# More loads ahead, twelve transfers on another queue, and one multiplication earlier: a recurrent-attention and two-layer kernel on one core

## The chip, the core and the metric

The kernel runs on one core of a Trainium2 chip. The metric is device time in microseconds (us), less is better. A core has five engines that matter here: TensorE (PE) multiplies matrices; VectorE (DVE), ScalarE (ACT) and GpSimd (POOL) do elementwise work; SyncE (SP) does nothing here but issue transfers. Each engine takes its instructions strictly in the order in which the program gives them to it, and waits at semaphores for the others.

## The reference, cut to what matters

Four sequences of 768 steps with 8 heads of width 48 go through a linear attention with a decaying state, and its output (3072 tokens of 384 features) through two feed-forward layers:

```python
for t in range(S):                                   # S = 768
    cur = einsum('bhd,bhe->bhde', u * k[t], v[t])
    y[t] = einsum('bhd,bhde->bhe', r[t], state + cur)
    state = w * state + einsum('bhd,bhe->bhde', k[t], v[t])
x = y as (3072, 384)
x = (sigmoid(x @ w_gate) * (x @ w_val)) @ w_out      # 384 -> 1536 -> 384
x = relu(x @ w_in) ** 2 @ w2_out                     # 384 -> 2048 -> 384
```

The layers' weights are float64. The kernel turns each of them into float32 parts on the chip.

## The kernel before, in words

**Steps and units.** The 768 positions are cut into six steps of 128, and step c of sequence b is a unit, n = 4c + b. There are 24. One unit's attention is a set of small matmuls with work around it: `attn_pre` (r times k times u, two POOL instructions, lines 232 and 233), `attn_prep` (k and r times powers of w, two DVE instructions, line 241), `attn_sum` (DVE), `attn_diag` (eight small ACT instructions, line 257), `attn_kh` (k times a table, one POOL instruction, line 264; from step 3 on DVE does it), `attn_mask` (DVE, line 328), `attn_mid` and `attn_state` (DVE, lines 403 to 414), and `attn_out`. `attn_out(n)` has the output matmuls of unit n, then the scores and the sums (k as `attn_kh` left it, times v) of unit n + 1, then two ACT copies of those sums (`us`, line 336) and two of the output (`ys`, line 384), and transfers of `ys` into `xr`, the layer's input (lines 386 to 392): two a unit, and four more at the last unit of a step, twelve a step. SP issues them.

**Phases.** Step 0's attention runs first, by itself. Then the first layer runs over step 0 for its first seven column blocks (phase 0), over steps 1 to 5 for all twelve, and over step 0 for the other five; then the second layer over all steps. While phase i runs, the attention of step i + 1 is woven in: `unit_ops` lays the operations of its four units into numbered slots, three to a column block, and `fill` runs the operations of one slot. A column block f is a gate product (`pg`), a value product (`pv`), line 445, and, one block later, an output product (line 464). Each phase starts with three ACT casts of `xr` (`xh`, line 432) and three DVE subtractions (`xl`, line 428).

**Weights.** 68 weight tiles of 384 KB are turned into float32 parts by `convert`. Call n does: an ACT cast and a POOL subtraction for tile n - 2 (lines 135 and 136), a DVE combination for tile n - 1 (line 148), an ACT and a DVE instruction on tile n (lines 156 and 158), and then asks SP for a tile that goes into the buffer which line 148 has just read. With `NRB` buffers that is tile n + NRB - 1. Four calls stand before phase 0, and in phases 0 and 1 nearly every slot ends with one.

**Order of loads.** SP's queue carries the loads too. A unit has four pieces, 1 MB together. At the start SP is given the units 0 to 4 and the weight tiles 0 to 3. Unit 5 (`B + 1`) comes after step 0's attention, and so behind step 0's twelve `xr` transfers on SP's queue. The units 6, 7 and 8 are asked for in `attn_out(4)`, behind the weight tiles that the calls of `convert` before it asked for.

Of the kernel before, what the change touches and what calls it, by code (L numbers as in the profile page):

```python
# [19 lines left out]
B, H, S, D = 4, 8, 768, 48  # L20
# [6 lines left out]
KT = DM // P  # L27
# [15 lines left out]
def tile_kernel(  # L43
# [18 lines left out]
    dp = ctx.enter_context(tc.tile_pool(name="dp", bufs=1, space=bass.MemoryType.DRAM))  # L62
    pp = ctx.enter_context(tc.tile_pool(name="pp", bufs=1, space=PSUM))

    NRB = 4
    NW = 36
    IN_W = 8
    CUT = 7
# [159 lines left out]
    def attn_pre(n):  # L228
        if n >= NU:
            return  # L230
        rn = rn_t[n]
        side(n).tensor_tensor(out=rn, in0=rn, in1=kv_t[n][:, HD:], op=ALU.mult)
        side(n).tensor_tensor(out=rn, in0=rn, in1=u_bc, op=ALU.mult)

    def attn_prep(n):
        if n >= NU:
            return
        two = trk.unsqueeze(2).to_broadcast([DP, HP, 2, L])
        for t in (k_t[n], r_t[n]):
            t = t.rearrange("p j (a t) -> p j a t", a=2)  # L240
            nc.vector.tensor_mul(t, t, two)
# [17 lines left out]
    def attn_kh(n):  # L259

        if n >= NU:
            return
        k = kv_t[n][:, HD:]
        side(n).tensor_tensor(out=k, in0=k, in1=th, op=ALU.mult)  # L264
# [75 lines left out]
    def attn_out(n):  # L340
        c, b = units[n]
        kv, am = kv_t[n], am_t.pop(n)
        opened.clear()

        def mm(a, q, j, m, lhsT, rhs):
            mm64(2 * a, q, (y1, y2)[a][64 * q : 64 * q + m, j * L : (j + 1) * L], lhsT, rhs)

        def reads(second):

            for j in range(HP):  # L350
                for q in range(2):
                    h = head(q, j)
                    a = h % 2 ^ second
                    o = slice(64 * (h % 2), 64 * (h % 2) + D)
                    if a or c:
                        st = mid_t[n][o, j] if a else state[o, b, j]
                        mm(a, q, j, D, st, r_t[n][o, j, a * L : (a + 1) * L])

        if n + 1 < B:
            attn_scores(n + 1)  # L360
        for j in range(HP):
            for q in range(2):
                h = head(q, j)
                for a in range(2):
                    x = slice(a * L, (a + 1) * L)
                    mm(a, q, j, width[q], kv[x, h * D :][:, : width[q]], am[x, h])
        reads(0)
        settle(kv)
        if n >= B:
            attn_scores(n + 1)  # L370
        if n != B - 1:
            attn_sums(n + 1)
        settle(kv)
        reads(1)
        while n >= B and len(kv_t) <= n + (4 if len(kv_t) < IN_W + 2 else 3) and len(kv_t) < NU:
            load_unit(len(kv_t))
        if n != B - 1:
            attn_us(n + 1)
        if b == 0:
            bank["y"] = sp.tile([P, B, HP, C], F32, tag="ys", name="ys", bufs=1)  # L380
            xraw[c] = sp.tile([P, KT, B, C], F32, tag="xraw", name="xr", bufs=1)
        ys = bank["y"]
        for a, y in enumerate((y1, y2)):
            nc.scalar.copy(ys[0:DP, b, :, a * L : (a + 1) * L], y[0:DP].rearrange("p (j t) -> p j t", j=HP))
        x = xraw[c]
        nc.sync.dma_start(out=x[0:48, :, b], in_=ys[0:48, b, 0:KT])
        nc.sync.dma_start(out=x[48:96, :, b], in_=ys[64:112, b, 0:KT])
        if b == B - 1:
            nc.sync.dma_start(out=x[96:128, 0], in_=ys[0:32, :, KT])
            nc.sync.dma_start(out=x[96:112, 1], in_=ys[32:48, :, KT])  # L390
            nc.sync.dma_start(out=x[112:128, 1], in_=ys[64:80, :, KT])
            nc.sync.dma_start(out=x[96:128, 2], in_=ys[80:112, :, KT])

    decay = wdec.unsqueeze(2).to_broadcast([DP, HP, D])

# [78 lines left out]
    def unit_ops(c, tiles):  # L474


        starts = (0, 9, 18, 27, 36) if tiles == F1 else (3, 8, 12, 17, 21)
        slots = [[] for _ in range(3 * tiles)]
        if c == 1:
            slots[0].append(lambda: (attn_pre(B + 1), attn_prep(B + 1)))  # L480
            slots[1].append(lambda: (attn_kh(B + 1), attn_sum(B + 1)))
            slots[2].append(lambda: (attn_diag(B + 1, 0), attn_diag(B + 1, 1)))
        for b in range(B):
            n = c * B + b
            ops = [
                lambda n=n: attn_out(n),
                lambda n=n: (attn_mask(n + 1), attn_mid(n + 1)),
                lambda n=n: (attn_state(n), attn_pre(n + 2)),
                lambda n=n: attn_prep(n + 2),
                lambda n=n: attn_sum(n + 2),  # L490
                lambda n=n: attn_diag(n + 2, 0),
                lambda n=n: attn_diag(n + 2, 1),
                lambda n=n: attn_kh(n + 2),
            ]
            s0, room = starts[b], starts[b + 1] - starts[b]
            for i, op in enumerate(ops):
                slots[s0 + i * room // len(ops)].append(op)
        return slots
# [114 lines left out]
    with tc.manual_schedule():  # L613
        nc.vector.memset(idle, 0.0)
        warm(WARM0)
        nc.vector.memset(seven, 0.0)
        nc.scalar.activation(seven, seven, AF.Sigmoid)
        nc.sync.dma_start(out=w_sb, in_=wt)
        id_sb = sp.tile([DP, D], F32, tag="ev", name="id_sb", bufs=2)
        maskf = sp.tile([C, L], F32, tag="ev", name="maskf", bufs=2)  # L620
        nc.sync.dma_start(out=id_sb, in_=ident)
        load_unit(0)
        nc.sync.dma_start(out=anti, in_=antid)
        nc.sync.dma_start(out=maskf, in_=mask)
        load_unit(1)
        load_unit(2)
        load_raw(0)
        load_unit(3)
        load_raw(1)
        load_raw(2)  # L630
        load_unit(4)
        load_raw(3)
        powers = tables()
        attn_pre(0)
        nc.gpsimd.tensor_copy(mask8, maskf)
        attn_pre(1)
        attn_prep(0)
        state_tables(*powers)
        attn_scores(0)
        attn_sum(0)  # L640
        attn_diag(0, 0)
        attn_diag(0, 1)
        attn_kh(0)
        attn_kh(1)
        attn_prep(1)
        attn_mask(0)
        attn_sum(1)
        attn_diag(1, 0)
        attn_sums(0)
        attn_us(0)  # L650
        attn_diag(1, 1)
        for n in range(B):
            m = n + 2
            if m < B:
                attn_pre(m)
                attn_kh(m)
                attn_prep(m)
            warm(WARM_OUT[n])
            attn_out(n)
            if m <= B:  # L660
                attn_mask(n + 1)
            if m < B:
                attn_sum(m)
                attn_diag(m, 0)
                attn_diag(m, 1)
            if n in (1, 2):
                convert()

        load_unit(B + 1)
        attn_pre(B)  # L670
        attn_kh(B)
        attn_prep(B)
        attn_sum(B)
        attn_diag(B, 0)
        attn_diag(B, 1)
        warm(WARM_X[0])
        attn_scores(B)
        attn_sums(B)
        attn_us(B)
        convert()  # L680
        convert()
        warm(WARM_X[1])
        for k in range(KT):
            x_from(0, k)
        attn_mask(B)
        attn_mid(B)
        for i, (layer, c, f0, f1) in enumerate(phases):
            ops = unit_ops(i + 1, f1 - f0) if i + 1 < NCH else []
            slot = 0

            def fill(f, j):

                nonlocal slot
                for op in ops[slot] if ops else []:
                    op()
                slot += 1
                lim = 0
                if i == 0:
                    lim = 3 * CUT + 2
                elif i == 1:  # L700
                    base = 3 * CUT + 2
                    lim = min(base + slot * (3 * F1 + 2 - base) // 27, 3 * F1 + 2)
                elif i == NCH - 1 and j < 2:
                    lim = min(3 * F1 + 3 * f - 2, 3 * F1 + 3 * CUT + 1)
                elif i == REDO and j < 2:
                    lim = 3 * F1 + 3 * f - 2
                elif i == REDO + 1 and j == 2:
                    lim = NWQ + 2
                for _ in range(2 if i == 0 and slot == 1 else 1):
                    if wn[0] < lim:  # L710
                        convert()

            for f in range(f0, f1):
                while (layer, f, 1) not in wunit:
                    convert()
                inner(i, f, fill)
        finish()
# [68 lines left out]
```

## Time and profile before

| | us |
|---|---|
| median of 3 runs | 977.85 (976.94 to 978.19) |
| the profiled execution | 979.93 |
| its span in the trace | 978.1 |
| PE busy in the span | 947.2 (97%) |
| DVE, ACT, POOL busy | 450.8, 402.9, 132.4 |
| transfers | 76.86 MB, mean 79 GB/s |

PE is busy for 97% of the span, but not evenly: its tenths in the first five of forty slices are 7, 7, 8, 8, 8, and DVE's 5, 6, 7, 7, 7 where the later slices have 3 or 4. [...] A row of the timeline gives the start, the duration, the engine, the line and the operation, and in brackets the time for which the engine stood idle before it and what released it.

### The profile page before, as it was taken

The numbers are of one execution on the slowest core, as the hardware profiler recorded it, in microseconds if no ns is written. First come the engines' busy times: TensorE is split into PE (matmuls) and PEld (weight loads), VectorE is DVE, ScalarE is ACT, GpSimd is POOL, SyncE is SP. The second block draws the span as 40 slices with busy tenths as digits, with TensorE's granted clock in tenths as the row PEclk, the third lists the DMA queues.
The fourth block names the chain that finished last, engine by engine and source line by source line (L and its number), as shares of the span: only waits on it lengthen the run. The fifth ranks groups of instructions, "written<-read, shape, count | busy, mean of one in ns | idle before, by whom it ended". The sixth has DMA issues, their size and how long they took to land.

```text
span 978.1 us, 16626 instructions
## 1 busy us (share of the span) xinstructions
PE 947.2 (97%) x6898; PEld 757.1 (77%) x6898; DVE 450.8 (46%) x742; ACT 402.9 (41%) x826; POOL 132.4 (14%) x121
## 2 busy tenths in 40 slices
PE   7788899999999999999999999999999999999997
PEld 4466678888888888887888888888888888888886
DVE  5677756754344345423344364433433433434332
ACT  3765565533333323322466463332422322323322
POOL 7455544200000000000133121000000000000000
PEclk7987999999999999999999999999999999999999
DMA  8674545532122222001244540010100100100000
GB/s 305 179 254 140 157 151 153 172 92 64 53 61 85 66 87 88 18 8 44 90 125 127 162 130 1 1 64 1 38 28 1 65 0 1 65 1 1 32 1 33
DMA packets 42235, 76.86 MB, mean 79 GB/s; under 512 B 5168, under 2 KB 17584, under 8 KB 42160
## 3 DMA queue, kind: packets, MB, share of 16 engines
q1 hardware_dynamic: 42160, 75.80, 24.5%
q8 instruction: 54, 0.88, 0.4%
q14 instruction: 21, 0.17, 0.1%
HBM read 60.05 MB, written 11.01 MB: 73 GB/s over the span
## 4 chain that ended last, share of the span: by engine, by line
PE 89%; DVE 2%; DMA 2%; POOL 2%; ACT 1%; SPq 1%; issue 1%; DVEq 0%; POOLq 0%; ACTq 0%
PE pg L445 35%; PE two L464 16%; PE pv L445 15%; PE po L464 12%; PE att L464 7%; PE att L272 4%; DMA first<-in_rkv 2%; SPq L104 1%; DMA xr<-ys 0%; POOL wu L136 0%; POOL gl L428 0%; ACT am L257 0%; ACT raw L156 0%; PE pw L611 0%; POOL first L264 0%
## 5 line engine op out<-in xcount | busy, mean ns | idle before, releaser
L445 PE MATMUL pg<-xh,wu 128*128 128x512 f32 x1008 | 318.3, 400 | 6.5 <-ACT wu L135 3.1
L445 PEld LDWEIGHTS pg<-xh,wu 128*128 128x128 f32 x1008 | 191.0, 190 | 55.6 <-ACT wu L135 3.6
L445 PE MATMUL pg<-xl,wu 128*128 128x512 f32 x504 | 196.7, 398 | 0.3 <-DVE xl L428 0.2
L597 ACT CAST gh<-s 128x512 fp32r<-128x512 f32 (+1 forms) x169 | 104.7, 620 | 192.5 <-DVE s L593 119.0
L596 DVE TENSOR_TENSOR s<-s 128x512 f32<-128x512 f32 (+1 forms) x97 | 66.6, 687 | 181.5 <-ACT s L595 181.5
L428 DVE TENSOR_TENSOR gl<-s,gh 128x512 fp32r<-128x512 f32 x162 | 111.5, 688 | 78.1 <-PE po L464 57.7
L464 PE MATMUL two<-gh,wu 128*128 128x512 f32 x472 | 147.3, 393 | 0.0
L445 PE MATMUL pv<-xh,wu 128*128 128x512 f32 x432 | 141.2, 408 | 1.5 <-POOL wu L136 1.4
L593 DVE TENSOR_TENSOR s<-pv,s 128x512 f32<-128x512 f32 x72 | 49.6, 689 | 197.4 <-PE pv L445 193.8
L595 ACT ACTIVATE s<-pg 128x512 f32<-128x512 f32 (+1 forms) x97 | 57.6, 594 | 190.4 <-PE pg L445 190.4
L445 PEld LDWEIGHTS pg<-xl,wu 128*128 128x128 f32 x504 | 95.9, 190 | 23.7 <-DVE xl L428 1.1
L464 PE MATMUL po<-gh,wu 128*128 128x512 f32 (+1 forms) x338 | 105.4, 392 | 0.0
L464 PEld LDWEIGHTS two<-gh,wu 128*128 128x128 f32 x472 | 88.8, 189 | 21.4
L445 PEld LDWEIGHTS pv<-xh,wu 128*128 128x128 f32 x432 | 81.4, 192 | 22.8 <-POOL wu L136 2.1
L464 PE MATMUL two<-gl,wu 128*128 128x512 f32 x236 | 92.5, 392 | 0.0
L579 ACT ACTIVATE s<-pg 128x512 f32<-128x512 f32 x72 | 43.8, 608 | 112.6 <-PE pg L445 112.5
L445 PE MATMUL pv<-xl,wu 128*128 128x512 f32 x216 | 86.1, 399 | 0.0
L464 PEld LDWEIGHTS po<-gh,wu 128*128 128x128 f32 x338 | 63.4, 188 | 14.8
L156 ACT ACTIVATE raw<-raw 128x384 bf16<-128x384 bf16 x68 | 73.6, 1082 | 0.0
L464 PE MATMUL po<-gl,wu 128*128 128x512 f32 (+1 forms) x169 | 66.2, 392 | 0.0
L464 PE MATMUL att<-gh,wu 128*128 128x512 f32 (+1 forms) x204 | 63.4, 392 | 0.0
L464 PEld LDWEIGHTS two<-gl,wu 128*128 128x128 f32 x236 | 44.2, 187 | 10.0 <-POOL gl L428 0.3
(298 smaller groups left out, 922.5 us busy)
## 6 DMA issues: line engine op xcount, KB each, us to landing
raw<-in_w SPq DMA_DIRECT2D x68, 384.0 KB, 3.1
kv<-in_rkv SPq DMA_DIRECT2D x16, 384.0 KB, 3.6
xin<-x2d SPq DMA_DIRECT2D x6, 768.0 KB, 4.2
out<-x2s SPq DMA_DIRECT2D x18, 256.0 KB, 2.1
first<-in_rkv SPq DMA_DIRECT2D x16, 256.0 KB, 5.5
kT<-in_rkv SPq DMA_DIRECT2D x16, 256.0 KB, 4.6
rT<-in_rkv SPq DMA_DIRECT2D x16, 256.0 KB, 5.0
x2d<-x2s SPq DMA_DIRECT2D x15, 256.0 KB, 2.0
```

Of the source, the lines that this page charges most:

```text
L104: nc.sync.dma_start(out=got[i][0], in_=got[i][1])
L156: nc.scalar.activation(top, top, AF.Prelu, scale=2.0**-112, alpha=2.0**32)
L272: nc.tensor.matmul(out, lhsT=lhsT, rhs=rhs, start=(bank, q) not in opened, stop=True, skip_group_check=True)
L428: (eng or nc.vector).tensor_tensor(out=dst, in0=src, in1=high.bitcast(F32), op=ALU.subtract)
L445: nc.tensor.matmul(ps, lhsT=a, rhs=b_, start=(i == 0), stop=(i == len(pairs) - 1))
L464: nc.tensor.matmul(po[k][:, ts], lhsT=a, rhs=b_[:, ts], start=(first and m == 0), stop=(last and m == 2 and ts is cuts[-1]),)
L579: nc.scalar.activation(s, pg, AF.Sigmoid)
L593: nc.vector.tensor_tensor(out=s[:, ts], in0=pv[:, ts], in1=s[:, ts], op=ALU.mult)
L595: nc.scalar.activation(s[:, ts], pg[:, ts], AF.Relu)
L596: nc.vector.tensor_mul(s[:, ts], s[:, ts], s[:, ts])
L597: nc.scalar.copy(gh[:, ts], s[:, ts])
```

## The change

The diff has four parts. Weight tiles get seven buffers in place of four, so `convert` asks for tile n + 6 in place of n + 3. The loads at the start take in unit 5 and the weight tiles 4, 5 and 6. Step 0's twelve `xr` transfers are issued from ScalarE's queue, in program order right behind the `ys` copies that they read; the other steps' stay with SP. And `attn_kh` of a unit moves ahead of its `attn_prep`: from the last of the unit's eight places in the slots to the fourth, one place behind `attn_pre`, and for unit 5 from slot 1 to slot 0.

```diff
-    NRB = 4
+    NRB = 7
...
         x = xraw[c]
-        nc.sync.dma_start(out=x[0:48, :, b], in_=ys[0:48, b, 0:KT])
-        nc.sync.dma_start(out=x[48:96, :, b], in_=ys[64:112, b, 0:KT])
+
+        eng = nc.sync if c else nc.scalar
+        eng.dma_start(out=x[0:48, :, b], in_=ys[0:48, b, 0:KT])
+        eng.dma_start(out=x[48:96, :, b], in_=ys[64:112, b, 0:KT])
         if b == B - 1:
-            nc.sync.dma_start(out=x[96:128, 0], in_=ys[0:32, :, KT])
...
+            eng.dma_start(out=x[96:128, 0], in_=ys[0:32, :, KT])
...
         if c == 1:
-            slots[0].append(lambda: (attn_pre(B + 1), attn_prep(B + 1)))
-            slots[1].append(lambda: (attn_kh(B + 1), attn_sum(B + 1)))
+            slots[0].append(lambda: (attn_pre(B + 1), attn_kh(B + 1), attn_prep(B + 1)))
+            slots[1].append(lambda: attn_sum(B + 1))
...
                 lambda n=n: (attn_state(n), attn_pre(n + 2)),
-                lambda n=n: attn_prep(n + 2),
+                lambda n=n: (attn_kh(n + 2), attn_prep(n + 2)),
                 lambda n=n: attn_sum(n + 2),
                 lambda n=n: attn_diag(n + 2, 0),
                 lambda n=n: attn_diag(n + 2, 1),
-                lambda n=n: attn_kh(n + 2),
+                lambda: None,
...
         load_raw(3)
+        load_unit(B + 1)
+        for n in range(4, NRB):
+            load_raw(n)
         powers = tables()
...
-        load_unit(B + 1)
         attn_pre(B)
```

## Rows read from the trace of the kernel before

**Rows 1.** Windows: stretch, length, busy us of PE to POOL, clock, DMA, GB/s.
```profile
22.17:37.31 15.14, 14.08 (x382) 8.83 (x380) 7.57 (x15) 14.21 (x46) 5.04 (x6) 1.00 0.39 104
37.31:117.81 80.50, 64.33 (x717) 49.56 (x717) 61.12 (x90) 47.43 (x105) 48.09 (x40) 0.85 0.67 208
117.81:130.00 12.19, 10.24 (x155) 7.37 (x156) 4.70 (x10) 5.08 (x16) 2.22 (x2) 0.86 0.28 91
130.00:450.00 320.00, 319.90 (x3166) 259.75 (x3165) 157.21 (x282) 125.65 (x304) 27.00 (x21) 1.00 0.27 81
```

**Rows 2.** Timeline of PE, rows ahead of which it stood idle.
```profile
46.23 0.50 PE L445 MATMUL pg<-xh,wu 128*128 128x512 f32 x1 [3.13 <-ACT wu L135]
48.09 0.79 PE L445 MATMUL pg<-xh,wu 128*128 128x512 f32 x1 [1.36 <-POOL wu L136]
...
72.21 1.09 PE L272 MATMUL att<-first 64*64 64x48 f32 x32 [1.88 <-POOL first L264]
...
89.75 1.09 PE L272 MATMUL att<-first 64*64 64x48 f32 x32 [3.88 <-POOL first L264]
...
124.66 0.67 PE L272 MATMUL att<-kv 64*64 64x48 f32 x32 [1.60 <-POOL kv L264]
```

**Rows 3.** Chain of waits that ended last: start, us, what.
```profile
37.86 4.85 DMA first<-in_rkv
...
53.53 6.11 DMA first<-in_rkv
...
111.78 4.79 DMA xr<-ys
...
125.63 3.82 PE pv L445 x9
...
139.94 2.10 PE pv L445 x9
```

**Rows 4.** Timeline of ACT: the first cast, and the `us` copies in phase 0.
```profile
37.31 1.73 ACT L432 CAST xh<-xr 128x512 fp32r<-128x512 f32 x3
...
55.35 0.54 ACT L336 COPY us<-att 112x192 f32<-112x192 f32 x2 [0.95 <-PE att L272]
...
73.97 0.54 ACT L336 COPY us<-att 112x192 f32<-112x192 f32 x2 [1.08 <-PE att L272]
...
91.51 0.54 ACT L336 COPY us<-att 112x192 f32<-112x192 f32 x2 [1.88 <-PE att L272]
...
108.84 0.54 ACT L336 COPY us<-att 112x192 f32<-112x192 f32 x2 [0.38 <-PE att L272]
```

**Rows 5.** Instructions on the tile `xr`: count, ns min/median/max, first and last start.
```profile
L387 SPq DMA_DIRECT2D xr<-ys x24: 594/599/1153, 24.1 to 447.3; - x24
```

**Rows 6.** Instructions on the tile `raw`, same columns.
```profile
L122 SPq DMA_DIRECT2D raw<-in_w x68: 327/328/1659, 10.1 to 576.8; - x68
```

**Rows 7.** Instructions of line 136, same columns: POOL's sequencer.
```profile
L136 POOLq EVENT_SEMAPHORE  x50: 17/17/330, 30.0 to 592.5; - x50
```

**Rows 8.** Timeline of DVE in phase 0.
```profile
42.73 2.43 DVE L241 TENSOR_TENSOR first<-first,trk 112x512 f32<-112x512 f32 x2 [0.73 <-DMA first<-in_rkv]
...
62.19 3.18 DVE L241 TENSOR_TENSOR first<-first,trk 112x512 f32<-112x512 f32 x2
...
98.79 0.68 DVE L241 TENSOR_TENSOR kT<-kT,trk 112x512 f32<-112x512 f32 x1
...
106.73 1.41 DVE L148 SCALAR_TENSOR_TENSOR wt__1405<-raw 128x384 int32<-128x384 int32 x1 [0.84 <-ACT raw L156]
```

**Rows 9.** Timeline of POOL: `attn_pre` of units 5 and 6.
```profile
42.19 1.03 POOL L232 TENSOR_TENSOR first<-first 128x384 f32<-128x384 f32 x1 [4.41 <-DMA first<-in_rkv]
...
59.70 1.26 POOL L232 TENSOR_TENSOR first<-first 128x384 f32<-128x384 f32 x1 [1.75 <-DMA first<-in_rkv]
```

**Rows 10.** Instructions of line 264 (`attn_kh`), columns as in rows 5.
```profile
L264 POOL TENSOR_TENSOR first<-first,th x8: 993/1008/1441, 13.5 to 88.4; 128x384 f32<-128x384 f32 x8
```

More of the change, by code (lines that the diff above doesn't have):

```diff
@@ L385, in attn_out @@
         x = xraw[c]
-        nc.sync.dma_start(out=x[0:48, :, b], in_=ys[0:48, b, 0:KT])
-        nc.sync.dma_start(out=x[48:96, :, b], in_=ys[64:112, b, 0:KT])
+        eng = nc.sync if c else nc.scalar
+        eng.dma_start(out=x[0:48, :, b], in_=ys[0:48, b, 0:KT])
+        eng.dma_start(out=x[48:96, :, b], in_=ys[64:112, b, 0:KT])
         if b == B - 1:
-            nc.sync.dma_start(out=x[96:128, 0], in_=ys[0:32, :, KT])
-            nc.sync.dma_start(out=x[96:112, 1], in_=ys[32:48, :, KT])
-            nc.sync.dma_start(out=x[112:128, 1], in_=ys[64:80, :, KT])
-            nc.sync.dma_start(out=x[96:128, 2], in_=ys[80:112, :, KT])
+            eng.dma_start(out=x[96:128, 0], in_=ys[0:32, :, KT])
+            eng.dma_start(out=x[96:112, 1], in_=ys[32:48, :, KT])
+            eng.dma_start(out=x[112:128, 1], in_=ys[64:80, :, KT])
+            eng.dma_start(out=x[96:128, 2], in_=ys[80:112, :, KT])
     decay = wdec.unsqueeze(2).to_broadcast([DP, HP, D])
```

## The prediction, made blind

> **What bounds the kernel now.** I read the windows first, then the rows ahead of which PE stood idle, the chain of waits, and last the timelines of ACT, DVE and POOL. From 130 to 450 us PE is busy for 319.9 of 320.0 us at the full clock [rows 1]; it runs matmuls that the change does not touch, and so do the windows behind. There nothing on another engine, no load and no place of `attn_kh` can move the end. What the change can win or lose lies ahead of 130 us. There PE is not the bound: phase 0, from the first cast `xh` at 37.31 [rows 4] to phase 1's first product at 117.81, takes 80.5 us, of which PE is busy 64.3, and at a mean clock of 0.85, with DVE busy 61.1 and POOL 48.1 [rows 1]. PE's gaps have names: block 1 waits for its weights, 3.13 and 1.36 us; the sums of units 6, 7 and 9 wait for `attn_kh`, 1.88, 3.88 and 1.60 us [rows 2]. But a gap of PE is worth only what the engine that feeds it next gives back, so the sum goes by the chain through DVE, ACT and POOL, not by adding PE's gaps.
>
> Step 0's attention has a bound of its own: between 22.17 and 37.31 ACT is busy 14.21 of 15.14 us [rows 1], and the first cast starts the moment ACT is through, without a wait [rows 4].
>
> **Step 0's transfers on ACT's queue.** Twelve issues leave SP and enter ACT, each right behind the `ys` copy whose result it sends. A transfer of this shape holds SP for 0.60 us (median of 24, shortest 0.594) wherever it stands [rows 5]. No row shows ACT issuing one. Bounds: at the least what a sequencer's own instruction takes, 0.017 us [rows 7], or 0.2 in all; at the most the longest such issue, 1.153 [rows 5], or 13.8. Between them lies a plain weight load's 0.327 [rows 6], or 3.9. I take 0.60, the same instruction on another sequencer: 7.2 us. ACT has 0.93 us of idle in the stretch (15.14 less 14.21) that can take some: +6.3 us on the first cast, which goes from 37.3 to about 43.6. What is queued behind the issues on ACT: the diagonals of units 2, 3 and 4, the `us` copies, the casts of the first weight tiles, and the three `xh`; `attn_mask` on DVE waits for the diagonals, PE for the masks. SP loses as much, but SP has nothing left there that is due.
>
> [...]
>
> [...]
>
> **Unit 5 and three weight tiles at the start.** Seven more transfers, 2.2 MB, go behind the others on SP's queue, so they delay none of the earlier ones. In the stretch behind, the DMA engines are used 39% at 104 GB/s [rows 1], so they land long before they are read. What goes is unit 5's load on the chain, 4.85 us [rows 3], for which POOL stood idle 4.41 us [rows 9] and DVE 0.73 [rows 8]. DVE then did two instructions in 2.43 us that take 0.68 each when undisturbed [rows 8]: 0.73 + 2.43 - 1.36 = 1.8 us earlier for the DVE work behind. POOL's share, `attn_pre(5)` and now `attn_kh(5)`, is done before phase 0 starts. Bounds: 0 (DVE is held up by another wait) to 4.5 (both PE gaps of block 1). I take 1.8, since DVE's order runs on. Late next: unit 6's load, which goes out behind weight tiles and takes 6.11 us [rows 3]; POOL waits 1.75 for it [rows 9].
>
> **Seven buffers** I cost at nothing: a load still waits for the same line 148, only three tiles further ahead. No wait for a weight tile stands in the rows; without that cover it is one issue, 0.33 us [rows 6], and a transfer.
>
> **`attn_kh` earlier.** The sums no longer wait for it, so `us` comes earlier. ACT was idle for PE ahead of `us` 0.95, 1.08, 1.88 and 0.38 us [rows 4], 4.3 in all; more than that PE's earlier finish cannot give ACT. Bounds: 0 to 4.3. I take all, since `attn_kh` or unit 5 stood behind each of them. Against it: each `attn_kh`, 1.0 us [rows 10], is now on POOL ahead of the weight subtraction and beside `attn_prep` on DVE. Such neighbours show a price: two of line 241 took 3.18 us, where alone one takes 0.68 [rows 8]. [...] Three units at 1.0 would be 3.0, nothing if the old price comes back whole; I take 2.0. In phase 0 then 1.8 + 4.3 - 2.0 = 4.1 us won, and phase 1's casts, which wait for SP's transfers of step 1 (4.79 us, [rows 3]), move with it, as those transfers follow the same chain.
>
> In phase 1 unit 9's `attn_kh` runs on an idle POOL. The gap of 1.60 [rows 2] goes, and with it, I think, the low clock behind: 3.82 less 2.10 for the nine products there [rows 3], 1.7. Together 3.3; bounds 1.6 and 3.3. From then on PE is the bound, so this counts in full. From phase 2 on, the move lies under full PE [rows 1]: nothing.
>
> **Sum.** +6.3 - 4.1 - 3.3 = -1.1 us: span 978.1 to 977.0. The profiled execution, 979.93, has 1.8 us around its span; the median of the runs, 977.85, lies 2.1 under it. I apply the difference to the median: 976.8.
>
> **Rivals.**
> 1. ACT's issues are cheap. For: a sequencer's own instruction takes 0.017 us [rows 7]. Against: SP's 0.60. At 0.017 the +6.3 vanishes: -7.4, 970.4. At 0.327: 3.9 - 0.9 = +3.0, so -4.4, 973.4. [...]
> 2. Slower: unit 6's load takes the place of unit 5's. Place: `attn_pre(6)` on POOL, 1.75 us idle already [rows 9]. If the chain gets there 1.8 + 0.95 = 2.75 us sooner but the load lands no sooner after the first cast than now (53.53 + 6.11 = 59.64 [rows 3] against 37.31, 22.3 us), POOL waits 4.5, the 2.75 are lost, and `attn_kh(6)` puts 1.0 more ahead of the weight subtraction that PE's next product needs. Phase 0 then gives 0.35 and the sum is +6.3 - 0.35 - 3.3 = +2.65: 980.5. If the low clock in phase 1 also stays, 982.2. It decides once phase 0 gives back less than 1 us. For: the load is asked for behind the same line 148 as before. Against: that instruction moves up too, and unit 5's megabyte no longer shares the engines with it.
> 3. ACT's issues are dearer than SP's: at 1.153 us the sum is +12.9 - 7.4 = +5.5, 983.3. Against: only one issue of that length.
>
> **How the numbers follow.** Chances: my forecast 0.47, by itself 974 to 979.5; rival 1 0.25; rivals 2 and 3 together 0.28. About 0.2% (2 us) is what a measurement of this kernel can tell from no change. Faster by more: rival 1 and 0.19 of the forecast's 0.47, 0.44. Within: 0.2 of the forecast and 0.05 of rival 2, 0.25. Slower: the rest, 0.31. The range takes in rival 1 at its cheapest and rival 2, and reaches towards rival 3: 970 to 983.
>
> **What would show it.** On ACT's queue, twelve transfers of `xr` at about 0.6 us each, the first `xh` at 43 to 45 us. Line 241 for unit 5 without a wait, two in about 1.4 us. No PE gap released by line 264 behind 40 us. POOL's wait ahead of `attn_pre(6)` no longer than 2 us (rival 2: over 4). From first `xh` to PE's start in phase 1 about 76 us in place of 80.5, and a clock above 0.86 in the twelve microseconds behind that. Wrong: `xh` before 40 us (rival 1) or after 47 (rival 3), or phase 0 that takes 80 us again.

## The result: 6.7 us slower, where 1 us faster was forecast

| | us |
|---|---|
| median before, 4 runs | 978.02 (976.94 to 980.15) |
| median after, 4 runs | 984.85 (983.1 to 986.72) |
| ratio | 1.0068 (95% interval 1.0047 to 1.0089) |
| profiled execution of after, its span | 984.52, 982.7 |

The time lies outside the range of the prediction, above it. The windows of after, cut at the places that answer to those of [rows 1] (first `us` copy, first cast `xh`, phase 1's first product, the 12.19 us behind it, the steady part); the clock column is the clock granted to PE, as a share of the full one:

```profile
23.03:47.29 24.26, 16.31 (x377) 10.33 (x380) 8.34 (x15) 14.27 (x46) 5.23 (x5) 0.86 0.59 180
47.29:124.87 77.58, 61.58 (x716) 45.59 (x716) 61.47 (x90) 46.84 (x105) 48.38 (x41) 0.91 0.62 194
124.87:137.06 12.19, 12.14 (x166) 8.90 (x166) 6.99 (x16) 7.11 (x20) 2.19 (x2) 0.86 0.35 111
137.06:457.06 320.00, 319.90 (x3165) 259.58 (x3164) 155.95 (x276) 123.19 (x301) 27.79 (x21) 1.00 0.27 81
```

Step 0's attention, from the first `us` copy to the first `xh`, takes 24.26 us in place of 15.14, at the same ACT busy time (14.27 against 14.21, [rows 1]): the twelve issues are not counted as busy time, but ACT computes nothing while it issues them. Phase 0 takes 77.58 in place of 80.50, and PE has hardly a gap in the 12.19 us behind it (12.14 busy, 10.24 before). The steady part has not moved.

ACT's timeline of after, from unit 2's second transfer to the first cast (`ACTq` is ACT issuing):

```profile
34.38 1.22 ACTq L389 DMA_DIRECT2D xr<-ys  x1
35.65 1.06 ACT L156 ACTIVATE raw<-raw 128x384 bf16<-128x384 bf16 x1 [1.96 <-issue]
36.45 0.72 ACT L384 COPY ys<-att 112x256 f32<-112x256 f32 x2
37.21 0.59 ACTq L388 DMA_DIRECT2D xr<-ys  x1
37.84 0.61 ACTq L389 DMA_DIRECT2D xr<-ys  x1
38.76 0.61 ACTq L391 DMA_DIRECT2D xr<-ys  x1
39.42 0.67 ACTq L392 DMA_DIRECT2D xr<-ys  x1
40.13 1.63 ACTq L393 DMA_DIRECT2D xr<-ys  x1
41.80 0.61 ACTq L394 DMA_DIRECT2D xr<-ys  x1
42.46 2.02 ACT L257 ACTIVATE am<-anti,dv 128x64 f32<-128x64 f32 x8 [5.28 <-DMA xr<-ys]
...
47.29 1.71 ACT L434 CAST xh<-xr 128x512 fp32r<-128x512 f32 x3
```

Eight of the twelve issues take 0.59 to 0.63 us, SP's price in [rows 5]; the others take 0.67, 0.69, 1.22 and 1.63, 9.1 in all. Between unit 3's second issue (done at 38.45) and the third ACT waits 0.31 us. The chain of waits says for what:

```profile
33.71 5.03 DMA xr<-ys
```

The issue at 38.76 was released by the landing of a transfer that ACT had itself asked for at 33.71. SP's waits between 10 and 60 us show that SP waits for ACT's transfers too (columns: who waited for whom, us in total, times, longest):

```profile
SPq L122 <- DMA xr<-ys: 14.7, 5, 6.2
```

The weight loads on SP now wait for ACT's transfers; the longest of these waits, 6.2 us, ends with tile 3's load. SP's timeline shows what that does to the early loads, first before, then after (weight tile 3, and in after unit 5 behind it):

```profile
17.79 0.33 SPq L122 DMA_DIRECT2D raw<-in_w  x1
```

```profile
26.49 0.33 SPq L122 DMA_DIRECT2D raw<-in_w  x1
27.12 2.83 SPq L104 DMA_DIRECT2D first<-in_rkv  x4
```

With the transfers left on SP the same two stand at 18.24 and 18.91. So in the changed kernel the loads added at the start are not early: they go out from 27.12 us on, and from 24 to 26 us the share of the DMA engines is 0.15, where it is 1.06 with the transfers left on SP.

In the compiled program 244 of the changed kernel's 293 transfers wait, besides for their data, for the completion of an earlier transfer, on one of eight completion semaphores; ACT's twelve use seven of the eight that SP's 281 use. With the transfers alone moved it is 228 of 293, all twelve of ACT's among them (four of its issues):

```
L387 DMA xr<-ys 48x3x128 [waits DMAHW6_49,Activation_49]
L388 DMA xr<-ys 48x3x128 [waits DMAHW0_49]
L390 DMA xr<-ys 32x4x128 [waits DMAHW2_49]
L391 DMA xr<-ys 16x4x128 [waits DMAHW4_49]
```

PE's rows that answer to [rows 2]:

```profile
48.02 3.11 PE L447 MATMUL pg<-xh,wu 128*128 128x512 f32 x6 [4.37 <-ACT xh L434]
57.33 0.50 PE L447 MATMUL pg<-xh,wu 128*128 128x512 f32 x1 [2.50 <-ACT wu L135]
74.02 0.50 PE L447 MATMUL pv<-xh,wu 128*128 128x512 f32 x1 [2.28 <-POOL wu L136]
106.61 0.79 PE L447 MATMUL pv<-xh,wu 128*128 128x512 f32 x1 [3.74 <-ACT wu L135]
```

No gap is released by line 264 (`attn_kh`) any more. But other gaps are there, released by the weights' cast and subtraction, with 3.74 us as the longest, where 3.88 by line 264 was the longest in [rows 2].

DVE and POOL at the start of phase 0, against [rows 8] and [rows 9], POOL's rows first:

```profile
47.68 1.11 POOL L232 TENSOR_TENSOR first<-first 128x384 f32<-128x384 f32 x1
48.87 1.34 POOL L233 TENSOR_TENSOR first<-first,u_bc 128x384 f32<-128x384 f32 x1
50.17 1.45 POOL L264 TENSOR_TENSOR first<-first,th 128x384 f32<-128x384 f32 x1
```

```profile
48.00 4.17 DVE L430 TENSOR_TENSOR xl<-xr,xh 128x512 fp32r<-128x512 f32 x3
...
54.99 1.28 DVE L241 TENSOR_TENSOR first<-first,trk 112x512 f32<-112x512 f32 x2
56.19 0.54 DVE L148 SCALAR_TENSOR_TENSOR wt__731<-raw 128x384 int32<-128x384 int32 x1
```

Line 241 for unit 5 runs without a wait, two in 1.28 us, as forecast. POOL's three instructions for unit 5 were not done early, though: they stand in its order behind the two weight subtractions of the prologue, and now run beside the three `xl` subtractions of DVE, which take 4.17 us, where before they took 1.90.

### The profile page after: what moved, and what is told of

Its sections match the earlier page's. It is cut to its first block, busy times and chain, and to the rows that moved or that the text cites. A ratio compares the mean times of both kernels' runs of the same rounds, so it can differ in the third digit from the quotient of the medians.

```text
span 982.7 us, 16600 instructions
## 1 busy us (share of the span) xinstructions
PE 944.7 (96%) x6892; PEld 753.8 (77%) x6898; DVE 452.5 (46%) x742; ACT 401.9 (41%) x826; POOL 133.6 (14%) x121
## 4 chain that ended last, share of the span: by engine, by line
PE 88%; ACT 4%; DVE 3%; DMA 1%; issue 1%; SPq 1%; ACTq 1%; POOL 0%; DVEq 0%; POOLq 0%
PE pg L447 35%; PE two L466 16%; PE pv L447 15%; PE po L466 12%; PE att L466 7%; PE att L272 4%; ACT am L257 1%; ACT raw L156 1%; DMA xr<-ys 1%; DVE first L241 1%; DMA first<-in_rkv 1%; DVE state L415 0%; ACT ys L384 0%; DVE mid L406 0%; ACT wu L135 0%
## 5 line engine op out<-in xcount | busy, mean ns | idle before, releaser
L257 ACT ACTIVATE am<-anti,dv 128x64 f32<-128x64 f32 x192 | 49.8, 335 | 13.8 <-DVE dv L247 5.8
```

What stands on the lines that cost most here:

```text
L257: nc.scalar.mul(am_t[n][:, h], anti, dv_t[n][:, h : h + 1])
```

## The experiments

All are compared with runs of the kernel before on the same chip. Differences in us are the ratio less one, times the median before (977.8 to 978.3).

**The transfers alone on ACT's queue.**

```diff
+        eng = nc.sync if c else nc.scalar
-        nc.sync.dma_start(out=x[0:48, :, b], ...)
+        eng.dma_start(out=x[0:48, :, b], ...)        # and the other five lines
```

> The kernel before with step 0's twelve transfers on ACT's queue and nothing else. Theory 1 (each issue holds ACT about 0.75 us, and ACT bounds step 0's attention): first xh 8 to 10 us later than in the kernel before, on ACT's queue 12 issues with a sum near 9 us; the whole slower by 6 to 9 us, less than the cast's delay because unit 5's load no longer stands behind these transfers on SP. Rival (the loads added at the start collide with ACT's transfers, the issues alone are cheap): first xh at most 4 us later, the whole within 3 us of the kernel before.

Measured: 986.57, ratio 1.0086 (1.0069 to 1.0103), +8.4 us. This is inside theory 1's range. The twelve issues take 7.8 us together; the first `xh` comes at 46.73, and ACT does no work for 5.39 us ahead of the diagonals behind the last six. There ACT also waits ahead of two of the last six issues, 0.99 us before 38.78 and 0.55 before 41.25:

```profile
38.78 0.61 ACTq L390 DMA_DIRECT2D xr<-ys  x1
...
41.25 0.59 ACTq L393 DMA_DIRECT2D xr<-ys  x1
```

This part alone accounts for the whole loss (6.7, and the intervals overlap).

**Only the first six of them.**

```diff
+        eng = nc.scalar if c == 0 and b < B - 1 else nc.sync
```

> The kernel before with only the six transfers of units 0 to 2 of step 0 on ScalarE's queue, the six of unit 3 on SyncE's as before. All twelve cost 8.4 us by themselves. Theory 1 (each issue holds ScalarE for its 0.59 to 0.70 us in a stretch where ScalarE has less than a microsecond to spare, so the cost goes with their number): six issues of about 0.63 us are 3.8 us, less 0.9 of idle time at most: 2.9 to 3.8 us slower than before, first cast xh 3 to 4 us later. Rival (only the six that stand directly ahead of the casts count, with the wait that they put ahead of the cast; the early ones are hidden, since ScalarE waits for TensorE there anyway): 0 to 1.5 us slower.

Measured: 983.42, ratio 1.0049 (1.0034 to 1.0064), +4.8 us. The cost goes with the number of issues, 0.7 to 0.8 us for each; the early ones are not hidden, so the rival is refuted. It is above the upper end of theory 1's range, which held issue time alone.

**ACT held for the same time, without transfers.**

```diff
+        for _ in range((6 if b == B - 1 else 2) if c == 0 else 0):
+            nc.scalar.copy(spare, spare)
```

> The kernel before, all transfers on SyncE's queue, with twelve extra copies of a spare tile of 128x512 on ScalarE (0.57 us each, by the casts xh of that shape) where the twelve issues stood: two behind each of units 0 to 2, six behind unit 3. They compute nothing that is used. Theory 1 (ScalarE's own time is the whole cost: 12 x 0.57 = 6.9 us less 0 to 0.9 of idle time): 6 to 7.5 us slower than before, about 0.9 of the 8.4 that the issues cost. Rival (a third or more of the cost is the second queue: waits for completion lanes and transfers that land later): 4 to 5.5 us slower.

Measured: 983.37, ratio 1.0055 (1.0041 to 1.0069), +5.4 us; the first `xh` at 42.92. The copies took 7.7 us in all, the issues 7.8. ACT's rows, six copies where the last six issues stood:

```profile
34.32 3.87 ACT L387 COPY spare<-spare 128x512 f32<-128x512 f32 x6
38.09 2.01 ACT L257 ACTIVATE am<-anti,dv 128x64 f32<-128x64 f32 x8
```

ACT goes from the copies to the diagonals in 3.87 us here, without a gap; with six issues in their place that was 5.39 us (transfers alone) and 5.28 (after). So about 5.4 of the 8.4 us is what holding ACT costs, and 3 us, by the difference, come with real issues; the two intervals touch, so the split is rough. The rival had the better size, but not all of the 3 us is waiting for the second queue. In the two traces 1.5 us of it are the two waits ahead of an issue, and 0.4 is one issue of 1.03 us; the rest is that an issue starts when the `ys` copy ahead of it has ended (unit 0's at 23.66 us, the copy's end at 23.62), where the spare copy starts a little before that (22.71 against 22.84).

**The change with the transfers left on SP.** It is the changed kernel with one line set back:

```diff
-        eng = nc.sync if c else nc.scalar
+        eng = nc.sync
```

> The changed kernel with step 0's transfers back on SP; loads and attn_kh as changed. Theory 1: first xh within 1 us of the kernel before (37.3), phase 0 shorter by 3 to 4 us, 2 us won in phase 1: 971 to 974 us, so 11 to 13 us less than the changed kernel. Rival (the slowness comes from the loads or from attn_kh's place): still above 978.

Measured: 977.81, ratio 1.0003 (0.9991 to 1.0016). The expectation was missed: the rest of the change isn't worth 4 to 7 us but nothing, and the first `xh` comes at 40.28, not within 1 us of 37.3. Some part of it costs.

**`attn_kh` earlier, alone.**

```diff
-                lambda n=n: attn_prep(n + 2),
+                lambda n=n: (attn_kh(n + 2), attn_prep(n + 2)),
...
-                lambda n=n: attn_kh(n + 2),
+                lambda: None,
```

(and unit 5's from slot 1 to slot 0, as in the change.)

> The kernel before with attn_kh moved alone. My prediction's terms: 4.3 less 2.0 in phase 0 and 3.3 in phase 1, 5.6 us in all; by what the changed kernel's trace shows rather 3 to 4: 973 to 975. [...]

Measured: 974.73, ratio 0.997 (0.9958 to 0.9982), -2.9 us (1.8 to 4.1 faster): the smaller size that was expected, and about half of the 5.6 of the prediction's terms.

**`attn_kh` earlier for unit 9 alone.**

```diff
+                lambda n=n: (n + 2 == 9 and attn_kh(9), attn_prep(n + 2)),
...
+                lambda n=n: n + 2 != 9 and attn_kh(n + 2),
```

> The kernel before with the multiplication of k for unit 9 alone two slots earlier, units 5 to 8 where they were. All five units together won 2.9 us. By the prediction's terms unit 9 wins the gap of 1.6 us and 1.7 us of low clock in phase 1, 3.3 us, and the others 2.3: then this kernel is 3 us faster than before and the others brought nothing. Rival (TensorE's order around the gap gives back part: only the gap itself goes, and units 5 to 8 won the rest): 1 to 1.6 us faster than before.

Measured: 975.86, ratio 0.9976 (0.9966 to 0.9985), -2.3 us (1.5 to 3.3 faster): between the two expectations, and by the medians' ratios most of the 2.9. The intervals overlap widely, so what units 5 to 8 bring can't be told from nothing by the times. PE's timelines show why it is so little. First the kernel with unit 9 alone moved, then the one with all five:

```profile
88.66 1.09 PE L272 MATMUL att<-first 64*64 64x48 f32 x32 [3.71 <-POOL first L264]
...
99.33 0.50 PE L445 MATMUL pv<-xh,wu 128*128 128x512 f32 x1 [0.38 <-POOL wu L136]
```

```profile
37.40 2.23 PE L445 MATMUL pg<-xh,wu 128*128 128x512 f32 x6 [0.92 <-ACT xh L432]
...
91.00 0.49 PE L445 MATMUL pg<-xh,wu 128*128 128x512 f32 x1 [0.46 <-POOL wu L136]
96.87 0.80 PE L445 MATMUL pv<-xh,wu 128*128 128x512 f32 x1 [3.74 <-ACT wu L135]
```

The gap of 3.71 us by `attn_kh` goes, and eight microseconds later stands a gap of 3.74 by the weights, where there was one of 0.38 (one product later). PE now does the work behind the old gap earlier, and waits for weights that come hardly earlier: ACT's cast of this tile starts 59.66 us behind the first `xh`, against 60.01.

**Buffers and early loads, alone.**

```diff
-    NRB = 4
+    NRB = 7
...
         load_raw(3)
+        load_unit(B + 1)
+        for n in range(4, NRB):
+            load_raw(n)
```

> The kernel before with seven buffers and the early loads alone. My prediction's term: 1.8 us. 975 to 977. Rival (unit 6's load takes the place of unit 5's, so nothing is won): 977.5 to 978.5. First xh unchanged by both.

Measured: 980.34, ratio 1.0024 (1.001 to 1.0038), +2.4 us: slower, against both theories. PE's timeline shows two gaps that before does not have, each in the middle of a group of like matmuls, with no releaser ("issue": it waited for nothing that the profile shows), and the window between them the count of what PE did (matmuls, weight loads):

```profile
26.99 0.63 PE L272 MATMUL pa<-first 48*64 48x64 f32 x28 [0.88 <-issue]
...
32.41 0.57 PE L272 MATMUL att<-am,first 64*48 64x64 f32 x25 [1.35 <-issue]
```

```profile
26.98:32.40 5.42, 3.75 (x127) 2.65 (x127) 3.96 (x8) 3.98 (x11) 0.00 (x0) 1.00 0.81 252
```

DMA in two-microsecond windows, first of this kernel, then of the one with `attn_kh` alone (the last two columns: share of the DMA engines, GB/s):

```profile
24.00:26.00 2.00, 2.00 (x50) 1.23 (x45) 1.31 (x3) 1.72 (x8) 1.92 (x3) 1.00 1.04 387
26.00:28.00 2.00, 1.12 (x67) 1.01 (x66) 0.90 (x2) 2.00 (x10) 0.67 (x1) 1.00 1.04 397
28.00:30.00 2.00, 1.90 (x66) 1.43 (x59) 1.78 (x4) 1.32 (x3) 0.00 (x0) 1.00 1.09 335
```

```profile
24.00:26.00 2.00, 2.00 (x64) 1.26 (x59) 1.44 (x3) 1.71 (x8) 1.92 (x3) 1.00 0.36 89
```

With the early loads the DMA engines are full to about 30 us (a share of 1.04 to 1.09 up to there, 0.45 behind), without them to about 23 (1.04 from 20 to 22 us, 0.80 from 22 to 24). The profiled executions are single ones, and their whole times don't follow the medians (978.04 here, 979.93 before): the stretches in which PE is granted half of the full clock fall differently in each (from 37.31 to 117.81 us the mean is 0.91 here, 0.85 before). So stretches are compared here, not spans.

**Unit 5 alone at the start; the three weight tiles alone at the start.** Half of the bytes each:

```diff
         load_raw(3)
+        load_unit(B + 1)                                   # the one
+        for n in range(4, NRB): load_raw(n)                # the other, NRB = 7
```

> The kernel before with unit 5's four loads alone at the start, four float64 buffers as before. Early loads of unit 5 and three weight tiles together cost 2.4 us. Theory F (TensorE's next instructions come over the same DMA engines as the loads, and come late while these are full; in the run with all loads TensorE stood 0.88 us at 27.0 and 1.35 us at 32.4 in the middle of a group of like matmuls, released by nothing, 127 matmuls and 127 weight loads apart): with 1.1 MB instead of 2.2 the DMA engines are full until about 26 us instead of 29, so at most the first of the two stalls remains and the load of unit 5 no longer makes block 1 wait: the same as before to 2 us faster. Rival (SyncE's queue: whatever goes out ahead delays the later transfers through the shared completion lanes, or unit 5's new place itself is bad for DVE and GpSimd): 1 to 2.5 us slower.

> The kernel before with seven float64 weight buffers and the three further weight tiles loaded at the start, unit 5 as before. Theory F (instructions late while the DMA engines are full): full until about 26 us, so at most the first stall, and nothing is won, as no weight tile was waited for: within 1 us of before. Rival (the tiles in themselves cost, through the order of the later loads and the shared completion lanes, whatever the DMA engines do): 1.5 to 2.5 us slower.

Measured: unit 5 979.46, ratio 1.0013 (1.0001 to 1.0026), +1.3 us; tiles 980.18, ratio 1.0018 (1.0007 to 1.0028), +1.8 us. In both, PE has the first gap and not the second, at the same matmul. First unit 5, then the tiles:

```profile
26.89 0.63 PE L272 MATMUL pa<-first 48*64 48x64 f32 x28 [0.70 <-issue]
```

```profile
27.38 0.63 PE L272 MATMUL pa<-first 48*64 48x64 f32 x28 [1.03 <-issue]
```

From the first to the last `us` copy of step 0 it is 12.23 us before, 13.10 and 13.23 here and 14.66 with all loads: 0.9, 1.0 and 2.4 more, where the medians' ratios give 1.3, 1.8 and 2.4. The stalls are as theory F had them; the times are above its ranges, and inside those of the rivals, which put the cost down to the order of the transfers. The times alone don't decide; the next two experiments bear on it.

**The three tiles at 27 us in place of the start.**

```diff
             attn_out(n)
+            if n == 1:
+                for i in range(4, NRB):
+                    load_raw(i)
```

> The kernel before with seven float64 weight buffers, the three further tiles asked for behind unit 1's output transfers, at about 27 us, instead of at the start (1.8 us slower there). Theory F (TensorE's fetches of instructions come late while the DMA engines are full): the stall moves with the load: none at 27 us, and one of up to 1.4 us at 31 to 33 us, at the second fetch, or none if it has been asked for by then; 0 to 1.5 us slower than before. Rival (the further tiles cost through something else that hangs on the seven buffers, not on the time at which they are loaded): 1.5 to 2.5 us slower with no stall of TensorE in the middle of a group.

Measured: 978.43, ratio 1.0005 (0.9994 to 1.0015). Seven buffers and three more tiles cost nothing that can be told when they are loaded here, as theory F had it and against the rival's 1.5 to 2.5; but the interval overlaps that of the tiles at the start (1.0007 to 1.0028). The gaps are small, though not quite where theory F had them: 0.40 us at the first place, ahead of the moved loads (in this run the engines were 0.91 full to 24 us), and 0.21 at the second.

**Ten more warm-up matmuls, with all early loads.**

```diff
-        warm(WARM0)
+        warm(WARM0 + 10)
```

> The kernel before with seven buffers and all early loads at the start (which has two stalls of TensorE, 0.88 us ahead of the third matmul of unit 3's scores and 1.35 us ahead of the eighth of unit 3's output), and ten more warm-up matmuls, with their ten weight loads, at the very start of TensorE's work, where it waits for data anyway. Theory F (pieces of the instruction stream of a fixed count): both stalls come ten matmuls earlier in the program, the first among the last matmuls of unit 2's output or the warm-up matmuls behind it, the second among the four warm-up matmuls ahead of unit 3's output, again 127 matmuls and 127 weight loads apart. Rival (the group's own data or a buffer): the stalls stay ahead of the third matmul of the scores and the eighth of the output.

One run, 979.15 against 978.6 for before; it was made for its trace. PE's timeline, and its count up to the first gap and between the two:

```profile
26.78 0.31 PE L272 MATMUL att<-first,us 48*48 48x64 f32 x3 [1.45 <-issue]
...
31.57 0.61 PE L611 MATMUL pw<-idle 128*128 128x512 bf16 x2 [0.48 <-issue]
```

```profile
0.00:26.77 26.77, 19.50 (x348) 11.23 (x348) 16.10 (x25) 9.87 (x35) 19.06 (x25) 0.87 0.91 328
26.77:31.56 4.79, 4.20 (x127) 2.74 (x127) 1.23 (x3) 4.43 (x16) 0.00 (x0) 1.00 0.84 267
```

Both gaps have moved nine matmuls up in the program, into other groups with other data, and stay 127 and 127 apart; the first stands behind 348 matmuls, against 347 without the extra ones. The place goes by the count of PE's instructions, and the rival is refuted.

**`attn_kh` earlier, and unit 5's load in a quieter place:** behind unit 2's output transfers, then behind unit 1's.

```diff
             attn_out(n)
+            if n == B - 2:                # then: if n == 1
+                load_unit(B + 1)
...
-        load_unit(B + 1)
```

> The kernel with k for the state multiplied in other slots alone (2.9 us faster than before), and unit 5's load moved to a stretch in which the DMA engines are nearly idle: behind unit 2's output transfers, ahead of unit 3's, at about 30 to 35 us. Theory (an early unit 5 is worth what block 1 waits for it; what cost in the changed kernel was only that the load stood in the full stretch): 1 to 2 us faster again, 971.5 to 974 by the median of 977.9 before. Rival (unit 5 is not on the path once k is multiplied elsewhere, or unit 3's output transfers are held up behind the megabyte): the same as with the slots alone to 1 us slower, 974.5 to 976.

> k multiplied in other slots, and unit 5's load behind unit 1's output transfers (SyncE stood idle there from about 27 to 29.5 us, and the DMA engines are free from about 24), instead of behind unit 3's. Theory: no output transfer is held up and the loads stand behind TensorE's first fetch of instructions at 27 us; unit 5's load no longer makes GpSimd wait 4.2 us in block 1: 1 to 2 us faster than with the slots alone (2.9 us faster than before), so 3.5 to 5 us faster than before. Rival (the megabyte at 27 to 30 us delays TensorE's second fetch, needed at about 31 us, by 1 us or more, as in the run with all loads at the start): TensorE idle without a releaser for 1 us in the middle of a group at 30 to 33 us, and no faster than with the slots alone.

Measured: behind unit 2's 977.24, ratio 0.999 (0.9979 to 1.0001), -1.0 us; behind unit 1's 973.83, ratio 0.9954 (0.9941 to 0.9968), -4.5 us. In the first, four issues of unit 5 stand on SP ahead of unit 3's six transfers, and the cast waits:

```profile
40.81 0.62 ACT L432 CAST xh<-xr 128x512 fp32r<-128x512 f32 x1 [3.23 <-DMA xr<-ys]
```

That eats more than it brings (-2.9 by `attn_kh` alone), as the rival had it, and 1 us beyond its range. In the second, PE has no gap without a releaser between 20 and 45 us, and the cast (37.20) does not wait; -4.5 is as the theory had it.

**As the last, and POOL's three instructions for unit 5 in the prologue,** ahead of its weight subtractions.

```diff
         attn_prep(B)
+        attn_pre(B + 1)
+        attn_kh(B + 1)
```

(and slot 0 keeps only `attn_prep(B + 1)`.)

> As the kernel with unit 5's load behind unit 1's output transfers and k in other slots, and GpSimd's three instructions for unit 5 issued in the prologue, ahead of the weight subtractions (GpSimd is idle there from 27 to 34.7 us), instead of in block 0. Theory (GpSimd's 3 to 4.5 us for unit 5 stand ahead of the weight subtractions that block 1's product waits for, 2.4 us in the run with the slots alone, and beside DVE's first three subtractions of the casts): 1 to 2 us faster than that kernel, 4.5 to 6.5 us faster than before. Rival (ScalarE's cast of the weights comes last for block 1, released by DVE, not GpSimd): no difference to that kernel.

Measured: 973.09, ratio 0.9951 (0.9935 to 0.9967), -4.8 us: no difference to the last kernel that the runs can tell. The three `xl` subtractions on DVE, first in the last kernel, then here:

```profile
37.92 4.18 DVE L428 TENSOR_TENSOR xl<-xr,xh 128x512 fp32r<-128x512 f32 x3
```

```profile
39.25 1.90 DVE L428 TENSOR_TENSOR xl<-xr,xh 128x512 fp32r<-128x512 f32 x3 [0.44 <-ACT xh L432]
```

With POOL's three instructions out of the way they take 1.90 us again. In the one profile phase 0 is 3.0 us shorter for it (73.1 against 76.1, from first cast to first cast), which the times of five and six runs don't bear out. This and the last are the versions that beat both kernels, by 4.5 to 4.8 us the kernel before. The next bound is in its PE timeline, the same weights:

```profile
95.67 0.49 PE L445 MATMUL pv<-xh,wu 128*128 128x512 f32 x1 [3.74 <-ACT wu L135]
```

## Why the prediction was wrong

**The sum.** Alone, the parts measure +8.4 (transfers), +2.4 (loads and buffers) and -2.9 (`attn_kh`), +7.9 in all; the change measures +6.7 (4.6 to 8.7). The prediction had +6.3 for the transfers and -7.4 for the rest. In the change itself the transfers are worth 6.4 us (1.0068 less 1.0003) and the rest +0.3. So by this split nearly the whole miss lies in the rest: early loads and an earlier `attn_kh`, forecast to win 7.4 us, won nothing that can be told. That +6.3 meets 6.4 is in part luck, as what follows on both shows.

**ACT's issues, +6.3 against +8.4 alone.** That issues on ACT go straight to the end was right, and so was the price of most of them (0.60 taken, 0.59 to 0.69 in ten of twelve). The first cast came 10.0 us later, not 6.3, and 9.1 of that lie in step 0's attention: the issues took 9.1 us in place of 7.2, two of them 1.22 and 1.63, with waits and pauses between them. Left out was that an issue waits for completion semaphores that both queues share: the chain's 5.03 us from an issue to a landing, 0.31 us of waiting here, 0.99 and 0.55 with the transfers alone. "SP has nothing left there that is due" failed as well: tile 3's load had still to go out, and behind it those that the change adds. They went out from 26.49 us on, and in the changed kernel PE doesn't stand for them; so the 6.4 is, by these rows, the transfers' own cost less what the early loads cost elsewhere.

One issue is small beside its transfer (0.6 of 5.03 us), but on an engine with 0.93 us to spare [rows 1] twelve issues took 9.1 us.

Rival 1 (cheap issues) is refuted. Rival 3's sum, 983.3, and its sign, `xh` after 47 (it came at 47.29), come near, but not by its mechanism: no issue but two was over 0.7 us.

**Early transfers costed at nothing, against +2.4 alone.** This step failed by its reasoning. It asked who reads the loaded tiles ("they land long before they are read") and took the stretch from 22.17 us with its 39%, which is a mean over a stretch whose start is full. It did not ask who else uses the DMA engines. PE does, as the author reads the rows. Its stalls stand at a fixed count of its instructions, 127 matmuls and 127 weight loads apart; there is none of that kind before, one of 0.7 to 1.0 us with half the bytes, two with all (one of them, 1.28 us at the second place, in the change with the transfers on SP). In the changed kernel itself PE has none over 0.33; there the loads go out from 27.12 us on, and PE is late itself. The page of after has the queue that fits:

```profile
q8 instruction: 54, 0.88, 0.4%
```

54 packets of 16 KB; 6892 matmuls and 6898 weight loads make 255 to a packet. The 254 between the two places come near that. The packets' own times in the traces bear the reading out. At all nine gaps without a releaser at the two places, from 0.21 to 1.45 us in six kernels, PE goes on 1.31 to 1.58 us behind the end of a 16 KB packet. Before, that packet ends at 24.16, and PE reaches the place at 26.3, late enough not to wait; with all the early loads it ends at 25.65, and PE goes on at 26.99. By that reading PE's instructions come in these packets, over the engines that the loads fill, and PE stands when a packet is late; no trace shows what a packet holds. That the place goes by the count, and that PE goes on at a nearly fixed time behind a packet, is shown; that the stalls are the whole of the 2.4 us is not, and that they vanish with the load in a quiet place rests on medians whose intervals overlap.

**Unit 5's load, 1.8 gained.** At the start it gained nothing that can be told: +1.3 alone, of which 0.9 is the stall. In a place without a stall, and with `attn_kh` moved, the medians' ratios give 1.6 more than `attn_kh` alone, though the two intervals overlap. The gain that was costed did come on line 241 (1.28 us without a wait, in place of 0.73 and 2.43), but DVE lost 2.3 at once, on `xl`. "POOL's share is done before phase 0 starts" was wrong in the changed kernel: it overlooked that unit 5's instructions stand in POOL's order behind two weight subtractions, which wait for ACT, and ACT is late. The first of the two starts at 45.38 us, after 18.67 us in which POOL stood idle for ACT's cast, and unit 5's first at 47.68, though its load had been asked for from 27.12 us on. So POOL's three instructions run beside `xl`. Done early in earnest, they brought 0.3, less than the runs can tell.

**`attn_kh`, phase 0: 4.3 less 2.0 won, against 0.6** (2.9 less 2.3, rough). This step failed. It took ACT's idle time ahead of `us` as the measure of what could be won. That ACT is idle there does not make `us` the thing that the next product waits for: that is the weights, through DVE's line 148 and ACT, and they come hardly earlier. The experiment's rows say it: behind PE's gap of 3.71 by line 264 the weights make PE wait only 0.38, without it 3.74. A gap that hides another is worth the difference. The 2.0 is a choice between 0 and 3.0 that no run shows by itself. What after shows in its place: line 241's two instructions take 2.88 us for unit 6, beside `attn_kh`, and 2.09 and 2.12 for units 7 and 8, against 3.18, 2.12 and 2.12 before; and line 148, which took 1.40 and 1.41 us beside the `attn_kh` of units 6 and 8 in the old place, takes 0.56 both times. So there the old price came back, and no new one shows. Phase 0 of the profiled execution before was also a long one: 79.33 us from its first cast to that of phase 1, where eight profiles of kernels with the same `attn_kh` have 77.0 to 78.9. Five of the kernels with all five units moved have 75.7 to 76.8, about a microsecond less.

**Phase 1: 3.3 won, against 2.3** (1.5 to 3.3). The half of it that is the gap was right: the gap by line 264 is gone, and PE is busy 12.14 of 12.19 us. The half that is the low clock was not. The sign was a clock above 0.86 in that stretch, and it is 0.86 in both. The nine products take 2.30 us in place of 3.82 [rows 3], but the stretch at half of the full clock only moved, onto other matmuls. A window of after, columns as in [rows 1]:

```profile
127.10:130.30 3.20, 3.18 (x56) 1.98 (x56) 2.07 (x4) 1.55 (x6) 0.85 (x1) 0.50 0.02 5
```

Three products of this size take 1.28 us at a clock of 0.50 and 0.70 at 1.00 in the kernel before, which is 1.8 times as long.

**PE's low clock at the start of phase 0** has no term in the sum. It came, and nothing is what it cost as far as the rows show. The first six products before, against 3.11 us after:

```profile
38.06 2.24 PE L445 MATMUL pg<-xh,wu 128*128 128x512 f32 x6 [0.92 <-ACT xh L432]
```

They take 0.9 us longer (PE is granted 0.50 from 48.5 to 51.8 us), but behind them PE still waits 2.50 us for block 1's weights. These come 10.0 us behind the first cast, against 8.9 before (46.23 less 37.31, [rows 2, 4]), and not for PE's sake: they hang on DVE, which runs from `xl` at 48.00 to line 148 at 56.19 without a wait, 2.3 us longer on `xl` than before.

**Rival 2** (unit 6's load) did not come: POOL waits 1.78 us for that load in after, as before (1.75, [rows 9]), not over 4.

## What to carry to other kernels

Price an issue on a compute engine at what an issue costs wherever it stands (0.60 us on SP here, 0.59 to 0.69 in ten of twelve on ACT), and add what either queue will wait for (0.31 to 0.99 us on ACT, 6.2 on SP); on an engine with less slack than that (0.93 us), it goes straight to the end (+8.4 us). Where the queues wait for each other, look at what stands behind the wait on the first one: here the loads that were to be early. A load that nobody waited for was not free here while the DMA engines were full: it cost 2.4 us at the start, with PE standing 0.88 and 1.35 us. Put it into a quiet stretch (a share of 0.14 from 26 to 28 us, behind unit 1's transfers, where PE had no such gap), and where it holds up nothing on its own queue either (behind unit 2's transfers the cast waited 3.23 us). A gap in front of one engine is worth only what the next wait behind it leaves: move it on paper, and look at which wait then ends last.

## What had not been expected of the hardware

- TensorE standing 0.21 to 1.45 us in the middle of a group of ready matmuls, at places 127 matmuls and 127 weight loads apart, in or behind stretches in which the DMA engines are full (343 to 401 GB/s), and none in the kernel before, where they run at 24 to 78 GB/s in that place. It goes on 1.31 to 1.58 us behind the end of a 16 KB packet of the queue that the page calls `instruction`.
- Single issues on ScalarE that take 1.03 to 1.63 us in place of 0.6. SyncE has such issues too with one queue alone (1.153 us, [rows 5]); no run here shows why.
